# Fixing VectorE's order, moving attention steps and changing the start in a fused attention and Strassen MLP kernel

## The chip, the cores and the metric

One core of one Trainium2 chip. The metric is the device time of one execution in microseconds (us), as the median of several. All timed runs here were in the fast state (none more than 1.5% above the fastest of its kernel). Most single executions of one kernel differ by about 0.3%, which is 3 us, a few by more (e9's slowest lies 0.8% above its fastest), so whatever is smaller than that is read from the traces, stage by stage, and not from the time. The granted clock, below, is the share of TensorE's full clock that the profile records: 1.00 is full, 0.50 is half.

## The reference, cut to what matters

```python
# q, k, v: (8, 8, 576, 64); w_in: (512, 2048); w_out: (2048, 512)
kv  = np.einsum('bhsd,bhse->bhde', k, v)
out = np.einsum('bhsd,bhde->bhse', q, kv)
rms = np.sqrt(np.mean(out * out, axis=-1, keepdims=True) + 1e-06)
x   = (out / rms * g_norm)              # then reshaped to (4608, 512)
h   = x @ w_in
g   = np.maximum(0.01 * h, h)
return g @ w_out
```

The 4608 rows of x are worked off in nine blocks of 512. Block 0 goes through plain products. Blocks 1 to 8 use Strassen's scheme (seven products instead of eight, with sums of quarters of the operands), and the inner sums of weights for blocks 2 and later are made during block 1. Attention for the next batch is cut into steps that are put between the products.

## The kernel before

Five engines run beside each other: TensorE (PE) multiplies, VectorE (DVE), ScalarE (ACT) and GpSimd (POOL) prepare and empty, and SyncE (SP) issues most DMAs. A bank (h_a, h_c, o_a) is a place where TensorE leaves products and which another engine has to empty before TensorE may fill it again; the 5.7 us wait below is a wait for a bank. The parts that the change and the argument touch, with cuts marked:

```python
pin = tc.keep_in_program_order         # what isn't pinned, the scheduler may reorder

def first_attention():
    keep_warm(2)                       # products of zeros, only to keep TensorE's clock up
    ...
    for j in range(3):
        load_w(j)                      # by SyncE's queue: w_in's first part (j = 0) and
                                       # second, 4 DMAs each, and one DMA of w_out
    for p in range(NP):
        ...                            # turn q by products with the identity
        keep_warm()
        ...
    for m in range(2):
        attention_kv(0, m, kv_ps)      # the two halves of kv
        if m == 0:
            keep_warm()
    copy_kv(0, kv_ps)
    ...
    outputs(0, N2, NT, 1, sums[1], ps, spare)
    divide(N2, NT, sums[1], spare)     # x = out / rms
    for j in range(1, 5):
        round_w(j)

def combine(c, part):                  # weight sums for blocks 2 and later
    ...
    eng = nc.vector if part == 2 else nc.gpsimd
    for js, y in parts[part]:
        t = view(stage, next(stage_homes) * NW, 4, len(js), P)   # three buffers, in turn
        ...
        add(eng, s1, y21, y22)         # not pinned
        add(eng, s2, s1, y11, True)
        ...
        pin(nc.sync.dma_start(to[:, 3:, :, :], t))

def product_h(c, w_sides, x_sides, to):   # block 1: one chunk of h, seven products
    def done(i, bank):
        ...
        elif i == 2:
            add(nc.vector, g11, bank, g11)     # not pinned
            relu(g11)
        ...

steps.update((i, a1) for a1 in [attention(1, False)]
             for i in (12, 13, 15, 16, 18, 20, 21, 23, 24, 26, 27, 28))
```

The last tuple says between which products of block 0 the twelve steps of batch 1's attention stand: four turnings of q with the two halves of kv, the kv copy, then two output steps and a division for each of two parts of x.

## Time and profile before

| | |
|---|---|
| time, median of 3 | 952.39 us (951.76 to 953.89) |
| span of the profiled run | 950.0 us |
| TensorE busy | 923.1 us, 97% |
| longest wait of TensorE | 5.7 us, at 171 us |
| TensorE's first product with w_out (o_acc) starts | 37.09 us |
| block 1 begins (first h_a) | 151.69 us |
| block 1, chunk 0 is done, first o_a | 178.81 us |
| first product of block 2 (h_ha) | 247.67 us |

The last four rows are start times of named groups on TensorE. As the order of TensorE's instructions hardly changes, the distance between two such anchors is the duration of a stage, and two kernels can be compared stage by stage.

Two stretches that the prediction tells without showing them, as TensorE's instructions of the kernel before, in order of time. The columns are start, duration, engine, line, operation, output and inputs, the partitions and shape, count, and in brackets the idle time before the group and what ended it. First the end of the first attention:

```profile
14.32 1.29 PE L112 MATMUL kv_ps<-v_in,k_in 64*64 64x64 f32 x72
15.55 1.13 PE L112 MATMUL idle_ps<-g 128*128 128x512 f32 x2
16.60 1.28 PE L112 MATMUL kv_ps<-pairs 64*64 64x64 f32 x72
```

The two kv halves take 1.3 us each at full clock, with a zero product (two instructions) between. Then the stretch that the moved attention steps are about:

```profile
107.83 1.16 PE L112 MATMUL o_ps<-qT,kv 64*32 64x448 f32 x12 [1.59 <-DVE kv L282]
109.18 0.94 PE L112 MATMUL o_ps<-qT,kv 64*32 64x448 f32 x4 [0.19 <-DVE qT L362]
110.05 3.70 PE L112 MATMUL h_ps<-xT,w_all 128*128 128x512 f32 x8
```

The output products wait for the kv copy and once more for a turned q, and from their start to the next h product 2.22 us pass (107.83 to 110.05).

### The profile page before, as it was taken

Reading aid. Unit: us, or ns where it says so; the run is one execution under the profiler, and the core shown is the slowest. Engines: PE = TensorE matmul, PEld = TensorE weight load, DVE = VectorE, ACT = ScalarE, POOL = GpSimd, SP = SyncE. Lnnn points to the kernel's source line nnn. Section 1 sums busy time; section 2 is a strip of 40 time slices with the busy share of each in tenths; the row PEclk is TensorE's granted clock in tenths of the full one; section 3 lists DMA queues with packets and bytes.
Section 4 is the critical chain, followed back from the end, with each engine's and each line's share of the span. In section 5 each row is a group of like instructions: output and inputs, shape, how many; then the busy total and the mean of one; then the engine's idle time right before and its main releaser. Section 6 shows DMA issues by size and latency. Waiting matters only on the chain.

```text
span 950.0 us, 17608 instructions
## 1 busy us (share of the span) xinstructions
PE 923.1 (97%) x6878; PEld 771.3 (81%) x6878; DVE 598.7 (63%) x1001; ACT 330.7 (35%) x671; POOL 318.5 (34%) x316
## 2 busy tenths in 40 slices
PE   8899999799999999999999999999999999999997
PEld 4444346688997889889998999889988999999996
DVE  3975894378355965477557855785568754565454
ACT  3633532233224422343234323432335223223321
POOL 1000353678822162116222622254223622432222
PEclk9999999899999999999999999999999999999999
DMA  8998924866499558965787578767855676667632
GB/s 252 236 247 202 242 79 154 275 200 216 149 275 312 182 164 247 311 203 180 238 269 244 177 220 297 242 181 210 287 175 175 184 222 184 192 194 215 182 120 89
DMA packets 90194, 200.03 MB, mean 211 GB/s; under 512 B 9856, under 2 KB 42112, under 8 KB 90112
## 3 DMA queue, kind: packets, MB, share of 16 engines
q1 hardware_dynamic: 79968, 187.70, 66.2%
q10 hardware_dynamic: 9856, 10.62, 3.4%
q8 instruction: 55, 0.90, 0.4%
q0 software_dynamic: 288, 0.59, 0.2%
q14 instruction: 27, 0.22, 0.1%
HBM read 172.39 MB, written 26.48 MB: 209 GB/s over the span
## 4 chain that ended last, share of the span: by engine, by line
PE 79%; DVE 10%; DMA 7%; ACT 1%; issue 1%; POOL 1%; SPq 0%; ACTq 0%; DVEq 0%; POOLq 0%
PE o_a L112 21%; PE o_c L112 16%; PE h_ha L112 9%; PE h_hc L112 8%; PE h_hb L112 7%; PE h_hd L112 6%; PE h_a L112 3%; PE o_acc L112 3%; DVE g L448 2%; PE h_ps L112 2%; PE h_c L112 2%; PE o_ps L112 2%; PE kv_ps L112 1%; DMA q_in<-in_q_dram 1%; DVE o L448 1%
## 5 line engine op out<-in xcount | busy, mean ns | idle before, releaser
L448 POOL TENSOR_TENSOR gs<-g 128x512 f32<-128x512 f32 x64 | 80.3, 1275 | 451.9 <-ACT g L617 451.8
L448 DVE TENSOR_TENSOR o<-o_c,o 128x512 f32<-128x512 f32 x88 | 60.5, 687 | 114.2 <-PE o_c L112 112.9
L112 PE MATMUL o_a<-pairs,gs 128*128 128x256 f32 x512 | 121.1, 379 | 0.0
L448 DVE TENSOR_TENSOR o<-o_a,o 128x512 f32<-128x512 f32 x104 | 71.1, 683 | 77.0 <-PE o_a L112 77.0
L681 ACT COPY w_all<-h_ha 128x512 f32<-128x512 f32 x84 | 48.8, 581 | 200.6 <-PE h_ha L112 200.5
L617 ACT ACTIVATE g<-g 128x512 f32<-128x512 f32 x124 | 77.4, 630 | 112.9 <-DVE g L448 110.2
L112 PEld LDWEIGHTS o_a<-pairs,gs 128*128 128x128 f32 x512 | 93.0, 190 | 10.3
L112 PE MATMUL h_ps<-xT,w_all 128*128 128x512 f32 (+1 forms) x136 | 60.1, 586 | 5.9 <-DVE xT L342 5.0
L112 PE MATMUL o_a<-w,g 128*128 128x256 f32 x256 | 61.2, 382 | 3.8 <-DVE o L448 3.6
L112 PEld LDWEIGHTS h_ha<-stage,w_all 128*128 128x128 f32 x448 | 58.0, 191 | 7.0 <-issue 2.4
L112 PE MATMUL o_a<-pairs,g 128*128 128x256 f32 x256 | 60.5, 379 | 0.0
L112 PE MATMUL o_c<-w,g 128*128 128x256 f32 x256 | 60.5, 379 | 0.0
L112 PE MATMUL o_c<-pairs,gs 128*128 128x256 f32 x256 | 60.5, 379 | 0.0
L112 PE MATMUL o_c<-w,gs 128*128 128x256 f32 x256 | 60.5, 379 | 0.0
L112 PE MATMUL h_ha<-stage,w_all 128*128 128x128 f32 x448 | 60.1, 277 | 0.0
L112 PE MATMUL o_acc<-w,g 128*128 128x512 f32 x128 | 57.9, 596 | 1.2 <-ACT g L759 1.2
L448 POOL TENSOR_TENSOR pairs<-w_all 128x512 f32<-128x512 f32 x8 | 10.2, 1271 | 137.3 <-ACT cut L216 109.0
L112 PEld LDWEIGHTS h_ps<-xT,w_all 128*128 128x128 f32 x136 | 26.2, 197 | 36.2 <-issue 26.3
L112 PEld LDWEIGHTS o_a<-w,g 128*128 128x128 f32 x256 | 46.3, 190 | 10.3 <-DVE o L448 3.5
L448 DVE TENSOR_TENSOR g<-g,pairs 128x512 f32<-128x512 f32 x84 | 52.8, 681 | 0.0
L448 DVE TENSOR_TENSOR w_all<-h_hc,w_all 128x512 f32<-128x512 f32 x56 | 38.4, 686 | 21.7 <-PE h_hc L112 18.5
L112 PEld LDWEIGHTS o_c<-w,g 128*128 128x128 f32 x256 | 46.5, 190 | 5.2
(151 smaller groups left out, 1975.4 us busy)
## 6 DMA issues: line engine op xcount, KB each, us to landing
w_all<-w SPq DMA_DIRECT2D x196, 448.0 KB, 4.2
pairs<-w SPq DMA_DIRECT2D x56, 512.0 KB, 4.4
out_dram<-o ACTq DMA_DIRECT2D x36, 256.0 KB, 2.7
v_in<-in_v_dram SPq DMA_DIRECT2D x30, 288.0 KB, 6.5
k_in<-in_k_dram SPq DMA_DIRECT2D x28, 288.0 KB, 5.7
q_in<-in_q_dram SPq DMA_DIRECT2D x56, 144.0 KB, 5.9
q_in<-in_q_dram SPq DMA_DIRECT2D x56, 140.0 KB, 5.8
w<-stage SPq DMA_DIRECT2D x12, 512.0 KB, 3.4
```

What stands on the lines that cost most here:

```text
L112: pin(nc.tensor.matmul(*args, **kw))
L448: eng.tensor_tensor(out_, a, b_, op=ALU.subtract if minus else ALU.add)
L617: nc.scalar.activation(t, t if src is None else src, func=AF.Prelu, alpha=SLOPE)
L681: nc.scalar.copy(q[:, at], banks[tag])
```

## The change

Its intent: keep VectorE from standing at a weight sum that nobody needs yet, bring attention steps to places where their inputs are ready, and shorten the start. The core of the diff, with cuts marked:

```diff
@@ start: w_in's first part by GpSimd's queue, no zeros between the turnings
+    load_w(0, nc.gpsimd)
...
-        for j in range(3):
+        for j in range(1, 3):
             load_w(j)
...
-            keep_warm()
@@ start: four products of zeros in front of h
         outputs(0, N2, NT, 1, sums[1], ps, spare)
+        idle = att_ps(NT, "idle_ps")
+        keep_warm(4)
         divide(N2, NT, sums[1], spare)
@@ VectorE's order in block 1
-    def add(eng, out_, a, b_, minus=False):
-        eng.tensor_tensor(out_, a, b_, op=...)
+    def add(eng, out_, a, b_, minus=False, pinned=False):
+        ins = eng.tensor_tensor(out_, a, b_, op=...)
+        if pinned:
+            pin(ins)
...
-            add(eng, s1, y21, y22)
+            add(eng, s1, y21, y22, pinned=part == 2)          # and s2, s3, s4
...
-                add(nc.vector, g11, bank, g11)
+                add(nc.vector, g11, bank, g11, pinned=True)   # and g21, g22
@@ attention steps
-                 for i in (12, 13, 15, 16, 18, 20, 21, 23, 24, 26, 27, 28))
+                 for i in (12, 13, 15, 16, 18, 20, 22, 23, 24, 25, 26, 27))
```

More of the change, by code (lines that the diff above doesn't have):

```diff
@@ L182, with load @@
                                 + [pair(i, NW) for i in range(4)])
-    def load(t, src):
+    def load(t, src, eng=nc.sync):
         if len(src.shape) == len(t.shape):
@@ L191, in load, with load_f64 @@
         for to, part in zip(t, src):
-            pin(nc.sync.dma_start(to, part))
-    def load_f64(src):
+            pin(eng.dma_start(to, part))
+    def load_f64(src, eng):
         a, n = src.shape[-2:]
@@ L197, in load_f64 @@
         raw = next(raw_homes).bitcast(U32).rearrange("p (n two) -> p n two", two=2)
-        load(raw.rearrange("p (a n) two -> p a (n two)", a=a), src)
+        load(raw.rearrange("p (a n) two -> p a (n two)", a=a), src, eng)
         return raw
@@ L235, with load_w @@
     w_raws = {}
-    def load_w(j):
+    def load_w(j, eng=nc.sync):
         dst, src = w_jobs[j]
         if w_in.dtype == I64:
-            w_raws[j] = load_f64(src.bitcast(U32))
+            w_raws[j] = load_f64(src.bitcast(U32), eng)
         else:
-            load(dst, src)
+            load(dst, src, eng)
     def round_w(j):
@@ L444, in first_attention @@
             round_w(j)
-    def add(eng, out_, a, b_, minus=False):
-        eng.tensor_tensor(out_, a, b_, op=ALU.subtract if minus else ALU.add)
+    def add(eng, out_, a, b_, minus=False, pinned=False):
+        ins = eng.tensor_tensor(out_, a, b_, op=ALU.subtract if minus else ALU.add)
+        if pinned:
+            pin(ins)
     def sides_w1(c):
@@ L517, in combine @@
             y11, y12, y21, y22 = (y[:, u, r, :, :] for u in range(2) for r in range(2))
-            add(eng, s1, y21, y22)
-            add(eng, s2, s1, y11, True)
-            add(eng, s3, y11, y21, True)
-            add(eng, s4, y12, s2, True)
+            add(eng, s1, y21, y22, pinned=part == 2)
+            add(eng, s2, s1, y11, True, pinned=part == 2)
+            add(eng, s3, y11, y21, True, pinned=part == 2)
+            add(eng, s4, y12, s2, True, pinned=part == 2)
             to = w1_dram[c][:, :, AT[js[0]]:AT[js[0]] + len(js), :]
@@ L650, in done @@
             elif i == 3:
-                add(nc.vector, g21, bank, g21)
+                add(nc.vector, g21, bank, g21, pinned=True)
                 relu(g21)
             elif i == 7:
-                add(nc.vector, g22, bank, g22)
+                add(nc.vector, g22, bank, g22, pinned=True)
                 relu(g22)
```

## The prediction

> **What bounds the kernel now.** I read the page first, then the waits of TensorE, then the stretches in which it waited, each in order of time. The page's busy row says where to look: TensorE (PE) is busy 97% of the 950.0 us span, every other engine far less.
>
> ```profile
> PE 923.1 (97%) x6878; PEld 771.3 (81%) x6878; DVE 598.7 (63%) x1001; ACT 330.7 (35%) x671; POOL 318.5 (34%) x316
> ```
>
> So only two things can shorten it: less work on TensorE, or fewer of its 26.9 us of waits (950.0 - 923.1) together with the half-clock stretches that long waits leave behind. The list of TensorE's waits names nearly all of them:
>
> ```profile
> PE h_a L112 <- ACT g L617: 5.7, 1, 5.7
> PE h_ps L112 <- DVE xT L342: 5.0, 2, 3.7
> PE o_a L112 <- DVE o L448: 3.6, 3, 1.8
> PE o_ps L112 <- DVE kv L282: 2.1, 2, 1.6
> PE idle_ps L112 <- DVE eps_sb L249: 1.5, 1, 1.5
> PE h_ha L112 <- DMA w_all<-w: 1.4, 1, 1.4
> PE o_acc L112 <- ACT g L759: 1.2, 1, 1.2
> ```
>
> The columns are total, count, longest, in us. The 5.7 us wait is single, and the costliest. Its stretch, VectorE (DVE) and ScalarE (ACT) in order of time, shows why (start, duration, instruction, idle time before it and what ended it):
>
> ```profile
> 162.00 0.69 DVE L448 TENSOR_TENSOR g<-h_a,g 128x512 f32<-128x512 f32 x1 [4.64 <-PE h_a L112]
> 167.78 1.46 DVE L448 TENSOR_TENSOR stage<-w_all 128x128 f32<-128x128 f32 x2 [5.08 <-DMA w<-stage]
> 169.16 0.68 DVE L448 TENSOR_TENSOR g<-h_c,g 128x512 f32<-128x512 f32 x1
> 169.88 0.63 ACT L617 ACTIVATE g<-g 128x512 f32<-128x512 f32 x1 [6.52 <-DVE g L448]
> 170.41 0.58 ACT L617 ACTIVATE g<-h_a 128x512 f32<-128x512 f32 x1
> 171.04 3.78 PE L112 MATMUL h_a<-xT,w_all 128*128 128x256 f32 x8 [5.70 <-ACT g L617]
> 174.62 2.63 PE L112 MATMUL h_c<-xT,w_all 128*128 128x256 f32 x8
> 177.09 1.89 PE L112 MATMUL h_a<-xt,pairs 128*128 128x256 f32 x8
> ```
>
> VectorE's next instruction is a weight sum for a later chunk, which needs a staging buffer still being written out by a DMA; until 167.8 us nothing behind it runs. Behind it stands the addition that empties bank h_c, then two activations, and the last of these frees bank h_a for TensorE. Then the restarted products are slow: 3.58 us and 2.47 us from start to start, where the next group takes 1.72 (177.09 to 178.81).
>
> The start is bound by a chain through VectorE. The chain of waits, in order of time, has no TensorE in it between 1.7 and 33.5 us:
>
> ```profile
> 1.73 8.21 DMA k_in<-in_k_dram
> 10.32 7.16 DMA stage<-in_moe_w_in_dram
> 17.59 0.67 ACT add L214
> 18.25 0.58 ACT cut L216
> ...
> 20.51 0.69 DVE w_all L223
> 21.20 0.67 DVE sum L312 x2
> ...
> 30.07 1.17 DVE xT L342 x2
> ...
> 32.80 0.70 DVE w_all L223
> ```
>
> **What the Trainium skill says.** "TensorE: Matmul & The Clock Gate", Part 1, says the array runs at half clock after about one idle window of 3.4 us and that the windows run freely. This trace agrees: the granted clock falls to 0.50 from about 169.4 to 176.1 us and from 26.0 to 29.2 us, each after an idle stretch over 3.4 us. The same page, "Architectural detail", says ACT and DVE are strict FIFOs. The trace agrees: the addition above needs nothing from the DMA and waits for it all the same. "DMA: Bandwidth & Descriptors", "Issuing engines are not separate DMA queues", says DMAs from SP, ACT and GpSimd share 16 engines, and another issuer saves only issue time. Here the eight first w_in parts take SP 9.54 us to issue (from 6.18), so issue time is what counts. "GPSIMD Engine Reference", Specifications, says GpSimd shares SBUF interfaces with VectorE when that reads two SBUF inputs. The trace agrees: a 128x256 sum took 0.42 us at 156 us with GpSimd idle and 1.38 us at 198.9 us beside it.
>
> **The change part by part.**
>
> *Order of VectorE in block 1.* The weight sums of one kind and the additions out of h's banks now stand in program order. In the built order, all eight sums of chunk 0 stand behind the first h addition, before the two later additions of chunk 0; chunk 1's sums stand behind chunk 1's first addition. So the sum that waited until 167.8 us is no longer in front of anything chunk 0 needs. TensorE finishes chunk 0's last product at 165.2; two activations remain (0.63 and 0.58 us), of which only the last must follow the product, so chunk 1 starts about 0.8 us later, at 166.0 instead of 171.04: 5.0 us. A gap of 0.8 us doesn't empty a window, so the clock stays up: (3.58 - 1.73) + (2.47 - 1.73) = 2.6 us more. Sum 7.6 us.
>
> *Attention steps moved.* One h product of 3.43 us now stands ahead of the first of batch 1's output products, which waited 1.59 us for the kv copy and 0.19 us for a turned q (107.8 and 109.2 us). The copy ended at 108.0, and the products would now be wanted at 106.2 + 3.4 = 109.7: 1.8 us gone. ScalarE gains too: its weight additions stood behind sums of those late products, so VectorE sat idle 1.98 us at 115.5 us, and that goes. Later TensorE waits 1.24 us (144.7 us) for activations of h which stand on ScalarE behind a root, which waits for VectorE. VectorE gets there earlier by that 1.98, by one weight sum (0.42, moved out of the stretch) and one sum of x (0.58, now behind it): 3.0 us. TensorE gets there 1.8 us earlier plus what the start gives. 3.0 - 1.8 = 1.2 us of slack against a wait of 1.24, so most of it goes, but it has to absorb the start's gain as well: I take 1.0. Sum 2.8 us.
>
> *Start.* w_in's first part by GpSimd's queue is issued after 3.2 us rather than 6.2 to 10.3 and should land near 12 (GpSimd's two transfers took 6.3 and 7.5 us). ScalarE's two steps are then done before the kv copy (17.96 to 18.45), and VectorE's 0.41 us of idle before its first rounding step (18.86) goes. Leaving out the four zero products (8 instructions; 1.05 us per pair, four of them: 4.2 us of TensorE) lets the q turnings end near 10.2 instead of 14.3. But k and v of pair 1 land at 13.5 and 13.3, those of pair 3 at 14.0 and 15.4, so kv's second half can't start before 15.4 where it started at 16.6. At most 1.2 us, less whatever the early w_in takes from the loads' bandwidth (0.5 MB at the 400 GB/s of that stretch is an estimated 1.3 us) and less a half-clock stretch if the 3.3 us hole from 10.2 to 13.5 fills a window. I take 0.3 + 0.4 = 0.7 us.
>
> *Four zero products in front of h.* They fill the 3.7 us in which TensorE waits for x (22.1 to 25.8; 4 x 0.86 = 3.4 us) and keep the clock at 1.00 for the first half of h, which took 3.6 us instead of 1.7. But the second half waits until 30.69 for VectorE's x in any case, and the next h until 33.55 for a rounded weight. Worth 0 on the path; it costs nothing as long as the clock is up when they run.
>
> Total: 7.6 + 2.8 + 0.7 = 11.1 us. After about 290 us the order on TensorE is unchanged.
>
> **The rivals.**
>
> *A new wait takes the place of the 5.7 us.* GpSimd: it is busy to 169.9 with chunk 1's sums in either kernel, then needs 5 us for g's sums, so it ends near 175.0, where before it then sat idle 6.88 us until TensorE came. TensorE arriving 7.6 us earlier takes just that. TensorE wants the first g sum near 178, and it is there at 173.7. VectorE: chunk 1's eight sums now run beside a busy GpSimd, 8.3 us at the slow rate instead of 2.8, then two turnings of q and a kv copy before the next h addition; I make that end at 184.2 where TensorE wants the bank at 184.8. Tight; a miss costs 1 us or so. A worse case, VectorE late in every chunk of block 1, would leave 947.
>
> *The gain of the start and of the steps is given back at 144.7 us.* If VectorE's stretch from 115 to 143 us doesn't move, TensorE reaches the same activations earlier and waits longer: the two parts together are then worth 1 us instead of 3.5, for about 945.
>
> *The start gets worse.* Without zero products between the turnings, the kv products may run at half clock, with the zero product between them at 1.7 us instead of 0.86; if the loads slip as well, kv ends 1 to 1.5 us later. The time becomes about 944.
>
> *Transfers set the pace anyway.* The DMA share is 0.93 from 260 to 280 us and TensorE waits 1.4 us for a weight there; arriving 10 us earlier could enlarge it by 1 us. In its favour speaks only that share; against it, that these loads follow TensorE's own progress.
>
> **Range and chances.** 952.4 - 11.1 = 941.3; I give back 0.9 for the tight places, which gives 942.2. All rivals but the worst stay within 938.5 to 948. Over 2% faster needs 933.3 or less, 19 us, more than two thirds of all of TensorE's waits: 0.02. Slower by 2% would need a new wait of 30 us, and no part of the order suggests one: 0.01.
>
> **What would show it right or wrong.** Right: no wait of h_a for ScalarE above 1 us in block 1's second part, no clock of 0.50 near 165 to 176, chunk 1's restart at about 1.73 us per group; no wait of the output products for kv near 107; the first h half at 1.7 us with the second half still starting near 30; VectorE's first rounding step right behind the kv copy. Wrong: a wait of h_a or h_c on VectorE's g in chunk 1, a longer wait of o_acc for ScalarE's g near 141 to 144, a half clock before the first kv products, or k and v landing well after 16 us.

## The result

| | before | after |
|---|---|---|
| median of 4 runs beside each other | 952.08 us (950.42 to 953.89) | 943.20 us (942.56 to 946.08) |
| ratio, 95% interval | | 0.9912 (0.9885 to 0.9940) |
| span of the profiled run | 950.0 us | 940.8 us |
| TensorE busy | 923.1 us | 919.2 us |

Ratios here and below are the mean time of one kernel's fast runs over that of the kernel before in the same rounds, so not quite the ratio of the medians that are quoted. The change is 0.9% faster, which is "within 2%"; 943.2 lies in the predicted range, 1.0 us above the predicted time.

The list of TensorE's waits after the change (total, count, longest, in us):

```profile
PE kv_ps L112 <- DMA k_in<-in_k_dram: 5.3, 2, 4.0
...
PE o_ps L112 <- ACT xT L317: 2.1, 2, 1.3
...
PE h_a L112 <- ACT g L623: 0.7, 1, 0.7
PE o_ps L112 <- DVE kv L283: 0.5, 1, 0.5
```

Against the list before (the lines left out are in both): h_a for ScalarE went from 5.7 to 0.7, the wait of o_acc is gone, o_ps for the kv copy went from 2.1 to 0.5. New are 5.3 us for k at the very start, and o_ps for ScalarE's xT with 1.3 us at the longest.

The place of the 5.7 us wait, after, all engines in order of time:

```profile
163.08 0.69 DVE L451 TENSOR_TENSOR g<-h_c,g 128x512 f32<-128x512 f32 x1 [0.96 <-PE h_c L112]
...
164.80 0.60 ACT L623 ACTIVATE g<-h_a 128x512 f32<-128x512 f32 x1 [0.37 <-PE h_a L112]
...
165.45 1.99 PE L112 MATMUL h_a<-xT,w_all 128*128 128x256 f32 x8 [0.69 <-ACT g L623]
```

No weight sum stands in front of the h_c addition; it runs as soon as TensorE is done with the bank. Only the last activation separates TensorE from its bank, and the next group takes 1.99 us where it took 3.78.

The start, after, on TensorE:

```profile
10.24 0.33 PE L112 MATMUL kv_ps<-v_in,k_in 64*64 64x64 f32 x2 [1.28 <-DMA k_in<-in_k_dram]
14.59 2.19 PE L112 MATMUL kv_ps<-v_in,k_in 64*64 64x64 f32 x70 [4.02 <-DMA k_in<-in_k_dram]
16.72 1.99 PE L112 MATMUL idle_ps<-g 128*128 128x512 f32 x2
18.64 1.28 PE L112 MATMUL kv_ps<-pairs 64*64 64x64 f32 x72
```

The q turnings are done early, but then TensorE waits 4.02 us for k, its granted clock falls to 0.50 (from 11.7 to 18.5 us), and the first kv half takes 2.19 us instead of 1.29, the zero product 1.99 instead of 1.13. The second half starts at 18.64 us, where it started at 16.60.

The stretch of the moved steps, after:

```profile
108.28 3.60 PE L112 MATMUL h_ps<-xT,w_all 128*128 128x512 f32 x8
111.81 0.98 PE L112 MATMUL o_ps<-qT,kv 64*32 64x448 f32 x16
112.72 3.70 PE L112 MATMUL o_acc<-w,g 128*128 128x512 f32 x8
...
129.70 0.70 PE L112 MATMUL o_ps<-qT,kv 64*32 64x128 f32 x16 [1.29 <-ACT xT L317]
```

With the h product ahead of them the output products run in one piece, 0.91 us from start to start instead of 2.22. Later, at 129.7 us, stands the new wait.

By stages, from the anchors of the two profiled runs:

| stage | before | after | difference | predicted |
|---|---|---|---|---|
| start to first o_acc | 37.09 | 39.30 | +2.21 | -0.7 |
| first o_acc to first h_a | 114.60 | 111.81 | -2.79 | -2.8 |
| first h_a to first o_a | 27.12 | 19.63 | -7.49 | -7.6 |
| first o_a to first h_ha | 68.86 | 68.66 | -0.20 | 0 |
| first h_ha to the end | 702.33 | 701.40 | -0.93 | 0 |
| span | 950.0 | 940.8 | -9.2 | -11.1 |

Two stages come out as predicted. Open are three things: whether these two have the predicted causes, whether the start really lost 2.2 us, and what the last 0.9 us are.

### The profile page after: what moved, and what is told of

The parts are those of the page before. It is cut to its first block, busy times and chain, and to the rows that moved or that the text cites. A ratio compares the mean times of both kernels' runs of the same rounds, so it can differ in the third digit from the quotient of the medians.

```text
span 940.8 us, 17607 instructions
## 1 busy us (share of the span) xinstructions
PE 919.2 (98%) x6878; PEld 770.2 (82%) x6878; DVE 600.4 (64%) x1001; ACT 331.0 (35%) x671; POOL 319.5 (34%) x320
## 4 chain that ended last, share of the span: by engine, by line
PE 87%; DVE 7%; DMA 3%; ACT 2%; issue 1%; ACTq 0%; SPq 0%; DVEq 0%
PE o_a L112 21%; PE o_c L112 16%; PE h_ha L112 10%; PE h_hc L112 8%; PE h_hb L112 7%; PE h_hd L112 6%; PE o_acc L112 5%; PE h_ps L112 5%; PE h_a L112 3%; DVE g L451 2%; PE h_c L112 2%; PE kv_ps L112 2%; PE o_ps L112 2%; DMA k_in<-in_k_dram 1%; DVE o L451 1%
## 5 line engine op out<-in xcount | busy, mean ns | idle before, releaser
L112 PEld LDWEIGHTS o_a<-pairs,gs 128*128 128x128 f32 x512 | 93.0, 190 | 10.3
L451 DVE TENSOR_TENSOR w_all<-h_hc,w_all 128x512 f32<-128x512 f32 x56 | 38.5, 688 | 21.7 <-PE h_hc L112 18.5
L112 PEld LDWEIGHTS o_c<-w,gs 128*128 128x128 f32 x256 | 46.5, 190 | 5.2
```

What stands on the lines that cost most here:

```text
L112: pin(nc.tensor.matmul(*args, **kw))
L451: ins = eng.tensor_tensor(out_, a, b_, op=ALU.subtract if minus else ALU.add)
```

## The experiments

Theory: the order of VectorE carries 7.5 us and the moved steps 2.8 us, independently of each other and of the start; the three changes of the start are worth nothing, and the 2.2 us of the pair of profiles are mostly chance in the landing of k and v. Rivals: the start is really 2 us worse and gives part of the gain back; the order matters only because a buffer was short; the gain of the steps is given back at the wait near 144.7 us.

All twelve kernels were correct. The runs of the kernel before that each group was compared with had medians of 953.33 us (e1 to e4), 952.82 us (e5 to e8) and 953.55 us (e9 to e12).

| run | median us, runs | ratio, 95% interval | kv copy at | first o_acc | o_acc to h_a | h_a to o_a |
|---|---|---|---|---|---|---|
| before (profile) | | 1 | 17.96 | 37.09 | 114.60 | 27.12 |
| changed (profile) | 943.20, 4 | 0.9912 (0.9885-0.9940) | 19.99 | 39.30 | 111.81 | 19.63 |
| e1 old start, zeros in front | 942.34, 4 | 0.9892 (0.9874-0.9910) | 18.84 | 38.34 | 111.81 | 19.62 |
| e2 zeros between turnings back | 941.98, 4 | 0.9882 (0.9866-0.9898) | 19.78 | 40.57 | 111.83 | 19.63 |
| e3 w_in on SyncE's queue | 942.47, 4 | 0.9889 (0.9874-0.9904) | 19.54 | 40.35 | 111.84 | 19.62 |
| e4 no zeros in front | 943.55, 5 | 0.9899 (0.9882-0.9916) | 22.66 | 42.63 | 111.82 | 19.63 |
| e5 order only | 946.50, 6 | 0.9933 (0.9907-0.9958) | 19.50 | 38.48 | 114.61 | 19.62 |
| e6 steps only | 950.46, 13 | 0.9980 (0.9967-0.9993) | 19.05 | 38.50 | 112.52 | 26.82 |
| e7 own buffer only | 951.90, 22 | 0.9989 (0.9979-1.0000) | 20.93 | 40.01 | 114.63 | 19.62 |
| e8 old start, zeros between halves | 941.67, 5 | 0.9883 (0.9864-0.9902) | 19.61 | 39.02 | 111.83 | 19.63 |
| e9 changed again | 943.12, 6 | 0.9901 (0.9876-0.9926) | 19.45 | 38.44 | 111.82 | 19.63 |
| e10 the two paying parts | 942.41, 6 | 0.9887 (0.9868-0.9906) | 21.19 | 40.17 | 111.81 | 19.63 |
| e11 zeros between halves, new start | 942.94, 6 | 0.9894 (0.9874-0.9913) | 19.71 | 38.69 | 112.29 | 19.62 |
| e12 second steps late | 944.42, 6 | 0.9910 (0.9888-0.9931) | 18.98 | 38.40 | 114.36 | 19.62 |

The last four columns are from each profiled run, in us. The two columns on the right hardly move between kernels with the same parts, 0.03 us in all but e11 (there TensorE stops for 0.5 us at 96.06 us, within the kv products of batch 1, until a load of v has landed); the two before them scatter by 2 us and more.

### The start (e1, e2, e3, e4, e10)

e1: the changed kernel with w_in on SyncE's queue and the zeros between the turnings, as before.

```diff
-    load_w(0, nc.gpsimd)
-        for j in range(1, 3):
+        for j in range(3):
             load_w(j)
+            keep_warm()                # after each q turning
```

> The changed kernel with the start of before: w_in's first part on SP again, a zero product after each q turning. Theory: the start of the change costs 2.2 us (first o_acc product at 39.30 us against 37.09) and the rest gains without it. Then the second half of kv starts near 16.6 us, the first o_acc near 37.1, and the time is 2.2 us under the changed kernel's 943.2, near 941.0. Rival: VectorE's stretch from 115 to 143 us sets when the o_acc product at 144.2 us may start, and an earlier start is waited away there: first o_acc near 37.1 but the product at 144.2 still near 144, time near 943.

e2 takes back only the zeros between the turnings (the last line of that diff), e3 only the queue of w_in (the lines above it).

> The changed kernel with only the zero products between q's turnings put back; w_in's first part stays on GpSimd's queue. Theory A (both parts of the start cost, and overlap: half clock about 0.9 us, late k and v about 1.1 us): clock 1.00 throughout, v of pair 3 still lands near 17.7, the second half of kv starts near 17.8 instead of 18.64, first o_acc near 38.4, time about 0.9 us under the changed kernel. Theory B (only the clock counts): first o_acc near 37.1, time 2.2 us under. Theory C (only the loads count): first o_acc near 39.3, same time.

> The changed kernel with only w_in's first part put back on SP's queue; no zero products between q's turnings. Theory A: k of pair 1 lands near 13.5 us, v of pair 3 near 15.4, but the clock is at 0.50 there, so the first half of kv and its zero product take 4.0 us instead of 2.3 and the second half starts near 17.6; first o_acc near 38.2, time about 1 us under the changed kernel. Theory B (only the clock): first o_acc near 39.3, same time. Theory C (only the loads): second half of kv near 16, first o_acc near 37.1, time 2.2 us under.

e4 takes away the four zero products in front of h:

```diff
-        idle = att_ps(NT, "idle_ps")
-        keep_warm(4)
```

> The changed kernel without the four zero products in front of h. Prediction's step: worth 0 on the path. The first half of h then runs at clock 0.50 and takes about 3.5 us instead of 1.97, but the second half still starts near 32.6 when x is there: first o_acc within 0.4 us of 39.30, time within 0.5 us. Rival (they pay): first o_acc later by 1.5 us or more, time 1.5 us up.

Measured: all four ratios lie between 0.9882 and 0.9899, with intervals of 0.2% on each side that overlap. No single change of the start shows in the time. The start positions that were expected did not come. kv's second half began at 17.48 us in e1 (16.6 expected), 18.42 in e2 and 18.18 in e3, and the first o_acc at 38.34, 40.57 and 40.35: none of the theories A, B and C of e2 and e3 fits, and e4's 42.63 is far outside its 0.4 us. e1's last o_acc group stands at 143.21 us, 0.96 earlier than the changed kernel's 144.17, just as its first stood 0.96 earlier: what the start gains or loses is passed on in full and not absorbed at 144 us. In the profiles the kv copy of e4 comes at 22.66 us, though e4 changes nothing in front of the kv copy: k landed later in that run (its first kv half waited until 16.26 us), and the second kv half ran at half clock (2.20 us). From the kv copy to the first o_acc e4 takes 19.97 us, 0.66 more than the changed kernel's profile.

e10 takes all three start changes away and leaves the order and the steps:

> Only the order of VectorE and the moved steps; the start with w_in on SyncE's queue and with zeros between the turnings, and no zeros in front of h. Theory (these two parts carry all the gain, and the three changes of the start are worth nothing together): ratio 0.988 to 0.990, within 0.2% of the changed kernel beside it; the first o_acc near 38.3 us, 111.8 us to h_a. Rival (the zeros in front of h keep the clock up and pay some 1 us; without them the first h is at half clock): the first o_acc at 39.5 us or later and a ratio 0.1% above that of the kernel with the old start and the zeros in front (0.9892).

Measured: 0.9887, in the range of the theory. Its first o_acc stood at 40.17 us, which is what the rival named, but not for the rival's reason: the kv copy came as late as 21.19 us, because TensorE stopped within the first kv half until 17.32 us (the trace names no releaser for these 2.13 us) and the second half then ran at half clock, 2.20 us; and from the kv copy to the first o_acc it took 18.98 us, less than the 19.50 us of e1, which has the zeros in front. So here the zeros in front of h are worth nothing; with e4's 0.66 us on the other side, the profiles leave their worth open within about 1 us.

e9, the changed kernel once more:

> The changed kernel as it is, timed beside the three others of this group. Theory: the start varies by about 2 us from run to run with the landing of k and v, so the single profile's 2.2 us of loss (first o_acc at 39.30 us against 37.09) is partly chance. Then the median is 942.5 to 944 and the ratio 0.989 to 0.991, and from the first o_acc on all distances repeat: 111.8 us to the first h_a of the second part, 19.6 us from there to the first o_a. Rival: the start always loses 2 us, and the first o_acc stands at 39 us or later again, with kv's second half not before 18.5.

Measured: 943.12 us, ratio 0.9901 (one of the six runs, 949.32 us, is far above the others). The first o_acc stands at 38.44 us, 0.86 earlier than in the first profile of the same kernel, and the later distances repeat to 0.01 us. So the start of one kernel scatters from run to run. To see what remains of the start's change, I take the first o_acc of all kernels with the old loads and the zeros between the turnings (before, e1, e5, e6, e7, e8, e10, e12): 37.09 to 40.17 us, median 38.49. The three with the new start and zeros in front (the changed kernel, e9, e11): 38.44 to 39.30, median 38.69. The difference of 0.2 us is far inside the scatter (with e4, which has the new start without the zeros in front, the median of four is 39.0 and the difference 0.5). The profile of the kernel before was the earliest of all: 1.4 of the 2.2 us come from there.

Why it was early can be read on TensorE. The first turning of q, in the kernel before and in e1:

```profile
5.24 1.23 PE L112 MATMUL q_ps<-ident,q_in 64*64 64x64 f32 x32
```

```profile
5.24 1.97 PE L112 MATMUL q_ps<-ident,q_in 64*64 64x64 f32 x32
```

e6, e8 and e12 have the slow form too (1.97 or 1.98 us), and in these four kv's first half starts 0.85 to 0.94 us later than in the kernel before. The recorded clock is 1.00 in both; why the turning is slower stays open. Besides, e2, e5, e7, e8 and e10 stop within kv's first half for 0.56 to 2.13 us, and the trace names no releaser. In e7 that stop lasts until 17.19 us, though k and v of this half had landed by 13.3. So the scatter of the old start is for the most part not one of landings, as the theory above had it.

The new start has two costs of its own, and the traces show them. The first is in the loads. The last load of v with the old queue (the kernel before), then in the changed kernel, with the w_in loads now ahead of it (KB each and us from issue to landing at the end of the line):

```profile
pairs<-in_v_dram SPq DMA_DIRECT2D x1, 288.0 KB, 10.2
```

```profile
stage<-in_moe_w_in_dram POOLq DMA_DIRECT2D x4, 128.0 KB, 9.3
...
pairs<-in_v_dram SPq DMA_DIRECT2D x1, 288.0 KB, 12.5
```

In the nine profiles with w_in on SyncE's queue this load takes 9.8 to 11.2 us and lands between 15.0 and 16.8 us; in the five with GpSimd's queue (the changed kernel, e2, e4, e9, e11) it takes 11.6 to 14.5 and lands between 17.0 and 20.2. kv's second half needs it: in e9 its first two products start at 17.62 us, and the rest wait for v until 18.15.

The second cost is the clock. In all five profiles without zeros between the turnings (the changed kernel, e3, e4, e9, e11) TensorE waits idle for k and the first kv half then takes 2.19 us, where it takes 1.28 in e1. From the end of that wait to the second half it takes 4.05 us in the changed kernel (14.59 to 18.64), 3.58 in e9 (14.04 to 17.62), 4.13 in e11 (14.22 to 18.35) and in e4, and 3.65 in e3, against 2.28 in the kernel before (14.32 to 16.60) and 2.26 in e1 (15.22 to 17.48). Set e9 against e1: TensorE is ready 1.18 us earlier, and the half clock takes 1.32 us back. The other profiles with the old start need 2.44 to 4.94 us between the halves, mostly because of the stops named above, and this hides the two costs in the medians.

### The order of VectorE, and the buffer (e5, e7)

e5: the kernel before with only the pinned additions.

```diff
+            add(eng, s1, y21, y22, pinned=part == 2)          # and s2, s3, s4
+                add(nc.vector, g11, bank, g11, pinned=True)   # and g21, g22
```

> The kernel before with only VectorE's order fixed in block 1; start and attention steps as before. Theory: this part carries most of the gain by itself. The wait of h_a for ScalarE's g falls from 5.7 us to under 1, the clock stays at 1.00 there, and from the first h_a of block 1's second part to the first o_a (27.12 us before, 19.63 us after) it takes 19.6 us; the wait at 144.7 us shrinks by about 0.4 because one weight sum leaves VectorE's stretch. Time 7.5 to 8.5 us under the kernel before. Rival: without the moved steps VectorE is too late elsewhere and the order pays less than 6 us.

Measured: 946.50 us, ratio 0.9933. From h_a to o_a 19.62 us instead of 27.12, so 7.50 us from this part alone. The timed difference, 6.3 us against the kernel before in the same rounds, is short of the 7.5 to 8.5 expected; its interval (0.9907 to 0.9958, 4 to 9 us) holds both. From o_acc to h_a it stays at 114.61, so the expected 0.4 us at the wait of 144.7 us did not come. Two lines of e5's waits show it, the old wait at 144.7 us still there and the 5.7 us one gone:

```profile
PE o_acc L112 <- ACT g L761: 1.2, 1, 1.2
...
PE h_a L112 <- ACT g L619: 0.7, 1, 0.7
```

e7: the kernel before, in the scheduler's order, but the last group of each chunk's sums gets a staging buffer of its own, so that no sum has to wait for the DMA that empties one.

```diff
+    stage4 = consts.tile([P, NW // 2], F32, name="stage4")
-            t = view(stage, next(stage_homes) * NW, 4, len(js), P)
+            t = view(stage4, 0, 4, 1, P) if js == (4,) else \
+                view(stage, next(stage_homes) * NW, 4, len(js), P)
```

> The kernel before, order not pinned, but the last batch of each chunk's weight sums has a staging buffer of its own, so that it need not wait for an earlier store of that buffer. Theory: the 5.7 us were the buffer's wait at the head of VectorE's queue. Then the wait goes without any pinning, and first h_a to first o_a takes about 19.6 us instead of 27.12, time 7 to 8 us under the kernel before. Rival: the unpinned order itself is at fault (later sums in front of earlier additions): the wait of h_a stays above 2 us.

Measured: the 5.7 us wait goes as with the order, 19.62 us from h_a to o_a. The time hardly moves, 951.90 us, ratio 0.9989. The gain is lost before block 2: from o_a to h_ha it takes 75.90 us instead of 68.86. VectorE of e7 where it is lost:

```profile
228.56 1.48 DVE L449 TENSOR_TENSOR stage<-w_all 128x256 f32<-128x256 f32 x1
229.96 1.48 DVE L449 TENSOR_TENSOR stage<-w_all,stage 128x256 f32<-128x256 f32 x1
231.37 0.81 DVE L449 TENSOR_TENSOR stage<-w_all 128x128 f32<-128x128 f32 x1
232.10 0.68 DVE L449 TENSOR_TENSOR o<-o_a,o 128x512 f32<-128x512 f32 x1
```

and TensorE:

```profile
232.83 3.30 PE L113 MATMUL o_a<-w,g 128*128 128x256 f32 x8 [3.37 <-DVE o L449]
235.92 2.31 PE L113 MATMUL h_c<-xt,pairs 128*128 128x256 f32 x8
```

No VectorE instruction waits for a DMA here. These three weight sums, and two of 0.89 us before them (226.32 and 227.74 us), are for later and slow beside a GpSimd that is busy all the time, and they stand in front of the addition that frees TensorE's bank o_a. TensorE waits 3.37 us and restarts at half clock: (3.09 - 1.73) + (2.15 - 1.73) = 1.78 us more, from start to start. With a wait of 1.63 us at 203.65 us for ScalarE's copy of o, that is 6.78 of the 7.04 us. So freeing the buffer does remove the 5.7 us wait, and a loss of the same size comes back at another place, where sums that nobody needs yet stand ahead of an addition that TensorE waits for. Such sums cost whether they wait or are only slow. One caution: e7 doesn't have the order of the kernel before at this place. There one sum of 0.43 us (230.51 us) stands between the addition to g and the next one to o from o_a, in e7 four do. The scheduler ordered anew, and no run frees the buffer in the old order.

### The attention steps (e6, e12)

e6: the kernel before with only the moved steps.

```diff
-                 for i in (12, 13, 15, 16, 18, 20, 21, 23, 24, 26, 27, 28))
+                 for i in (12, 13, 15, 16, 18, 20, 22, 23, 24, 25, 26, 27))
```

> The kernel before with only the attention steps moved. Theory: the waits of 1.6 and 0.2 us for the kv copy near 107 us go, and most of the 1.24 us at 144.7; a wait of about 1.3 us for ScalarE's xT near 130 us comes in, as in the changed kernel. From the first o_acc to the first h_a of the second part it takes 114.60 us before and 111.81 after: here about 112.2, time 2.4 us under the kernel before. Rival: without the freed VectorE the gain is waited away at 144.7 us, 114 us or more, time within 1 us of before.

Measured: 950.46 us, ratio 0.9980, 112.52 us from o_acc to h_a instead of 114.60: 2.08 us alone, against 2.79 us together with the order. The 0.7 us between have a place in e6's waits, in the one line of it for o_acc:

```profile
PE o_acc L112 <- ACT g L759: 0.5, 1, 0.5
```

The wait at 144 us is still there with 0.49 us. VectorE of e6 has a weight sum of 0.42 us at 126.37 us in the stretch that this wait hangs on; in the changed kernel the pinned order has moved it out. Those 0.42 us look like the reason, but e5 speaks against it: there too the pinned order has moved this sum out, and the wait stayed at 1.24 us (a VectorE instruction behind it, 1.25 us in the kernel before, took 1.46). So only the two parts together give these 0.7 us, and why stays open.

e12: the changed kernel with the old start (and e8's zeros between the halves), with the steps of the first part of x moved and those of the second part left at their old places.

```diff
-                 for i in (12, 13, 15, 16, 18, 20, 22, 23, 24, 25, 26, 27))
+                 for i in (12, 13, 15, 16, 18, 20, 22, 23, 24, 26, 27, 28))
```

> Old start, zeros between the halves, and of the attention steps only the first ones moved: those of the second part of x stay where the kernel before has them (one o_acc group later). Theory (the new wait of 1.29 us at 129.7 us comes from the second output step being one place earlier, so that its bank is still being read by ScalarE): that wait is gone, and the wait of o_acc for ScalarE's g near 144 us stays away because VectorE is early enough; from the first o_acc to h_a 110.5 us instead of 111.8, ratio 0.1% lower than the others. Rival (the later step puts ScalarE's g behind the root again): the wait of about 1.2 us near 144 returns, 111.8 us or more, same time.

Measured: my theory falls, and the rival's wait comes back twice as long as it named. e12's TensorE:

```profile
138.22 3.60 PE L112 MATMUL h_ps<-xT,w_all 128*128 128x512 f32 x8
144.37 8.54 PE L112 MATMUL o_acc<-w,g 128*128 128x512 f32 x16 [2.55 <-ACT g L768]
152.76 1.89 PE L112 MATMUL h_a<-xT,w_all 128*128 128x256 f32 x8
```

The new wait at 129.7 us is gone, as expected. Counted from the first o_acc, TensorE is 3.08 us ahead of the kernel before at the group of 111.82 us (73.42 against 76.50). But at 144 us it meets the same activations of h, which stand behind a root that waits for VectorE. It waits 2.55 us instead of 1.24, the clock falls, and the 16 products take 8.39 us from start to start instead of 6.97. Of the 3.08 us only 0.24 are left at h_a, and the time, 944.42 us, is 2.0 us above e10's in the same group (the intervals overlap; the stage is what shows it). The windows of e12 (stretch, its length, TensorE's busy time and count, granted clock, DMA share, GB/s):

```profile
143.50:144.00 0.50, 0.00 (x0) 0.84 1.02 324
144.00:144.50 0.50, 0.13 (x1) 0.50 1.01 287
...
147.00:147.50 0.50, 0.50 (x2) 0.75 0.00 0
```

So the place of the second part's steps decides this stage: with them late, all gain at 107 us is given back at 144 us; one place earlier they bring VectorE and ScalarE forward enough, at the price of the 1.29 us at 129.7 us.

### The half clock between the halves of h (e8, e11)

After the four zeros the first half of h is done near 29.5 us and TensorE waits 2.97 us for x. Both kernels add three zero products there, e8 with the old start, e11 with the new.

```diff
+        warmer.append(keep_warm)
...
+                    if n == 0 and part == 0:
+                        warmer.pop()(3)
```

> The changed kernel with the start of before (as e1) and three more zero products between h's first half and second half. Theory: in the changed kernel and in e1 to e3 the four zeros in front of h end the first half early, so that TensorE then idles 3 us and the half clock falls on the second half and the next product (0.50 from about 32 us on); filling that hole keeps the clock at 1.00 from 18 us on, and from the kv copy to the first o_acc it takes about 18.7 us (19.50 in e1, 20.8 in e2 and e3, 19.13 before). Time 0.8 us under e1. Rival: VectorE's rounded weight sets the start of the second h product, and the clock there is worth nothing: 19.4 us, time as e1.

> The changed kernel with three products of zeros between the two halves of the first h. Theory (the half clock after 32 us costs the second half of h and the first w_out products some 1.5 us, but VectorE's rounded weight sets most of that): the clock stays at 1.00 from 29 to 38 us and the first o_acc comes 0 to 0.5 us earlier relative to the kv copy than the changed kernel's 19.31 us, so 0.1% at most. Rival (the half clock is what costs): 1.5 us or more earlier, 17.8 us from kv copy to o_acc, ratio 0.15% lower than the changed kernel's beside it.

Measured: in both the clock stays at 1.00 from 28 to 38 us. From the kv copy to the first o_acc e8 takes 19.41 us and e11 18.98, where e1 takes 19.50, the changed kernel 19.31 and e9 18.99. The half clock there costs 0.3 us at most in these, as VectorE's rounded weight sets the next h product anyway. Only where the half clock lasted through two windows, in e2 and e3, did it cost more: 20.79 and 20.81 us. Whether it comes at all is not set by the length of the wait. The same wait of the same kernel, in the changed kernel's profile and in e9's:

```profile
32.00:34.00 2.00, 1.42 (x3) 0.54 0.40 57
```

```profile
32.00:34.00 2.00, 1.95 (x8) 1.00 0.40 121
```

Clock 0.54 in the one and 1.00 in the other, after an idle stretch of the same length. The times of the changes fit the freely running windows that the prediction names. In the changed kernel's profile it changes at 11.66, 18.49, 32.14 and 35.56 us: two, four and one times 3.41 us apart. In e9 it changes at 13.60 and 17.01. Carried on in steps of 3.41 us (an estimate), e9's windows end at 30.7 and 34.1 us, which cuts its idle stretch (29.1 to 32.05) into 1.6 and 1.4 us; in the changed kernel 2.5 of the 2.97 us lie within the window that ends at 32.14. The times, 0.9883 and 0.9894, are not told apart from those of the kernels without these zeros.

None of the twelve is shown to be faster than the changed kernel. The five that have both paying parts in full and all or part of the old start (e1, e2, e3, e8, e10: 0.9882 to 0.9892) do all lie below the four with the whole of the new queue and without zeros between the turnings (the changed kernel, e4, e9, e11: 0.9894 to 0.9912). The mean difference is 0.15%, an estimated 1.4 us, and less than the interval of any single ratio, so a loss by the new start is hinted at and not shown by the times.

## Why the prediction was right or wrong

*Order of VectorE: right, in cause and size.* Predicted 7.6 us, measured 7.50 alone (e5) and 7.49 together. Both terms are there: the wait went from 5.70 to 0.69 us, which is 5.0, and the restart of the two slow groups accounts for the rest. What the prediction did not say is that a free buffer removes the same wait without any order, and that this alone doesn't pay: e7 loses 7.0 us later, in an order of the scheduler's making. The tight place in chunk 1 held; the rival of a new wait there did not come (h_a to h_ha takes 88.29 us in every kernel with the order, 95.98 before).

*Attention steps: the total right, the terms wrong.* Predicted 1.8 + 1.0 = 2.8, measured 2.79. The first term was mis-sized: the waits of 1.59 and 0.19 us are gone, and the output products also run in one piece, 0.91 instead of 2.22 us; counted from the first o_acc, 3.08 us are gained there (73.42 against 76.50). A wait that the prediction missed takes some of it: 1.29 us at 129.7 us, where the second part's output products, now one place earlier, need a bank that ScalarE still reads; by the next h product TensorE is 1.7 us later than in e12, which has no such wait (94.57 against 92.85 us after the first o_acc). And the wait at 144.7 us goes whole, 1.24 us, not 1.0. The estimate that VectorE gets there 3.0 us earlier was good: the last activations before that wait start 104.2 us after the first o_acc instead of 106.99, 2.8 us earlier. But one of its terms, the 0.42 us for a weight sum moved out, brought nothing by itself in e5. The rival "given back at 144.7 us" is no idle one: e12 shows it in full, as soon as the second part's steps stay late. It was avoided by the last half of the step list, to which the prediction gave the smaller share of the gain.

*Start: wrong.* The step that failed is "I take 0.3 + 0.4 = 0.7 us". The 0.3 was for VectorE's idle time before its first rounding step. In the kernel before that step starts 0.90 us after the kv copy does, in the changed kernel 0.41, at once behind the copy. But in the eight other profiles with the old queue it is 0.40 to 0.51 as well, as kv came later there: the wait was one of an early run. The 0.4 was for an earlier second half of kv, and two costs that the prediction names itself took more than that. The early w_in delayed the last v, to 17.0 to 20.2 us instead of 15.0 to 16.8; the prediction's own estimate for this, 1.3 us, was already more than the 1.2 us that it had to gain. And its rival of kv products at half clock came true in every profile without the zeros: 1.3 to 1.9 us more between kv's halves than in the kernel before and e1. Measured in place of the 0.7 us gained: 2.2 lost in the pair of profiles, 0.2 lost between the medians of the eight and three starts, and nothing that the times resolve.

*Four zeros in front of h: right as far as the profiles resolve it.* Predicted 0. Without them e10 reaches o_acc 18.98 us after the kv copy and e4 19.97; with them the changed kernel and e9 take 19.31 and 18.99. The hole that they leave behind the first half of h, with a half clock in some runs, was not foreseen: that half clock costs 0.3 us at most where it lasts one window, and some 1.5 us more where it lasts two (e2 and e3).

*Transfers: the wait did not grow.* It fell from 1.39 to 0.27 us, which is more than the 0.93 us between h_ha and the end. But it varies whatever the change: 1.25 us in e2, 0.5 in e9, 1.69 in e10, none in e5, e6, e7 and e8. So those 0.9 us can't be put down to the change.

*The sum.* The two parts that can be measured exactly give 7.5 + 2.8 = 10.3 us (0.7 of it only together: the steps alone give 2.08), the start nothing or a loss. The timed difference is 952.08 - 943.20 = 8.9 us. The predicted 10.2 (11.1 with 0.9 given back) was off by the start's term, and by no more than two executions of one kernel differ.

## What to carry to other kernels

Where one engine serves both the critical path and work for later, fix its order so that the later work stands behind; in e7 a free buffer alone only moved the loss. Before a step is moved, look for the next place where TensorE meets an engine that the move didn't speed up: the gain is given back there unless that engine comes earlier too. A load that is started earlier can delay the loads that are wanted first. And take a stage of a few microseconds that waits for first loads from several profiles, as one profile can be 2 us off by itself.

## What the Trainium skill lacked or had wrong

- "TensorE: Matmul & The Clock Gate", Part 1, names one idle window of about 3.4 us as what halves the clock, and the table "Why this matters for your kernels" warns of gaps over about 3 us. In e12 TensorE's last product ended near 141.8 us (an end is modelled), the clock was 0.50 from about 143.8 to 147.25 us, and the whole gap was 2.55 us. So the clock fell 2.0 us into a gap shorter than a window. In the changed kernel's profile it fell 2.5 us into a wait of 2.97 us, and in e9's a wait of 2.97 us left it at 1.00. The way back agrees with the page's one busy window: 0.50 for about 3.4 us in e12, and for two windows, about 169.3 to 176.1 us, in the kernel before, where the products came back only at 171.04.
- "GPSIMD Engine Reference", Specifications, says that GpSimd and VectorE share SBUF interfaces, without giving a size there for sums of two inputs: a 128x256 sum took 0.42 us at 156 us in the kernel before with GpSimd idle, and 0.89 to 1.48 us in e7 from 226 to 232 us with GpSimd busy throughout. Not every sum pays: two took 0.43 and 0.41 us at 230.51 and 231.47 us in the kernel before, with GpSimd busy around them.
- "DMA: Bandwidth & Descriptors" has no figure for the spread of equal loads, or for what an earlier transfer costs those behind it: the last load of v, 288 KB issued at 5.0 to 5.7 us, took 9.8 to 11.2 us to land in the nine profiles with the old queue, and 11.6 to 14.5 us in the five where four w_in transfers of 128 KB had been issued before it.
